# A dilated sliding-window attention and mixer kernel: batch 1 loaded ahead of the second channel weight, the first channel weight in three tiles, scores over 64 rows

## The chip, the cores and the metric

The kernel runs on one core of a Trainium2 chip. The metric is the device time of one execution in microseconds (us). TensorE (PE) multiplies matrices and transposes, VectorE (DVE) and ScalarE (ACT) work on vectors and can read PSUM (the banks that PE writes), GpSimd (POOL) works on vectors in SBUF alone, and SyncE (SP) issues most transfers. POOL issues some transfers too, in the same order as its vector work. PE is fed by weight loads (PEld) that the profile shows as a row of their own.

## The reference

Eight batches, eight heads, 576 positions, 64 channels a head. The first four heads attend to the last 32 positions, the other four to every fourth of the last 128. The result, 576 x 512 for each batch, goes through a mixer over positions (256 hidden) and one over channels (1536 hidden):

```
scores = scale * np.matmul(q, k.transpose(0, 1, 3, 2))
mask_plain = (rel >= 0) & (rel < window)                    # window = 32
mask_dil = (rel >= 0) & (rel < window * dilation) & (rel % dilation == 0)   # dilation = 4
attn = softmax(where(mask, scores, -1e9));  x = attn @ v
h = np.maximum(xt @ w_tok1, 0.0) @ w_tok2                   # over positions
u = x + h.transpose(0, 2, 1)
h2 = np.maximum(u @ w_ch1, 0.0) @ w_ch2                     # over channels
return u + h2
```

## The kernel before, in words

**Attention.** The heads are taken in pairs, hp 0 and 1 plain, hp 2 and 3 dilated. A pair's keys lie transposed on 128 partitions (kt): 64 channels of one head, then 64 of the other. So do its queries, but in two copies (qz): copy h holds head h's rows and zeros in the other 64, so that a matmul over all 128 rows gives the scores of one head. Plain scores are made in blocks of 128 keys by 160 queries, dilated ones by residue modulo 4 in blocks of 128 by 128; the last 64 positions (512 to 575) are blocks of 64 columns of their own (sm). ACT takes exp from the bank to SBUF (attp, attd); the window is set afterwards by a multiplication on POOL with a constant 0/1 band (`mult(nc.gpsimd, ...)`), or, in batches 0 and 1 (`veiled`), ahead of the exp by a matmul that adds a large negative number (veil). The value step of a head multiplies with v and a column of ones, and DVE divides.

**Turning q and k.** In batches 0 to 2 PE transposes them (`transposes`). From batch 3 on (`by_dma`) SP issues transposing transfers to qta, kra and tta (the last 64 positions), and `place_steps` copies from there into qz and kt: POOL the plain pairs and the tails, DVE the dilated queries and a part of the dilated keys.

**Mixer.** `emit_h1` and `emit_u` make the mixer over positions, uT is u turned (by PE up to batch 2, by DMA after). `gen_main` is the channel mixer: 12 row blocks gp (four matmuls of 512 columns each, line 646), each followed by a relu on ACT or DVE to gt, then the second product yp (line 665, 12 matmuls of 256 columns for each half of a block of 128 positions). The last 64 positions of two batches are handled together in the odd batch (gt, line 637, and yp, line 685). The first channel weight is w3, one tile of 128 x 4 x 1536, loaded in three pieces of 512 columns; row block mb uses columns of piece mb // 4 only:

```
return w3[cb][:, 512 * (mb // 4) + mb % 4:512 * (mb // 4) + 512:4]
```

The second channel weight is w4, one tile in three contiguous pieces; yp uses all three in each group of 12 matmuls.

**Order.** The order of all instructions is written out. `interleave` runs the channel mixer of batch b and counts planner time, about a microsecond of PE a unit, on each piece of it and on each step's own cost; a step whose place has been reached is put in next. So a list such as `value_steps(b + 1, 0.4, 0.95)` places the value steps of batch b + 1 at 0.4, 1.35, ... of batch b's channel mixer. Scores are made two batches ahead (`score_steps(b + 2, 15.0 + late, 2.6)`), values, h1, u and uT one batch ahead. Each engine takes its instructions in this order. PSUM has eight banks: main0 to main2 in turn for gp, gt and yp, sc0 and sc1 in turn for scores, three called fl for value steps, h1, u and transposes.

**Start.** POOL loads w3 in three pieces (line 738) among its casts. After the preparation of batch 0, lines 851 to 871: `gate` is a one-element copy on POOL into the target of a load from what has to land first; the load waits for the copy. The first gate lets w4 (line 854) wait for a piece of w3, the second lets batch 1's q and k wait for w4's first piece:

```
gate(w4a[0:1, 0, 0:1], w3[0][0:1, 512:513])
...
gate(l32[(1, "t")][0:1, 0, 0:1], w4[0][0:1, 0:1])
...
```

Between the gates stand w4's three loads; behind the second, batch 1's tails, q and k on SP, its casts on POOL, then its v. Batch 1's transposes begin at planner time 12.6, its value steps at 20.3, its uT at 34.8; the first product of batch 0 ends at 10.3.

Of the kernel before, what the change touches and what calls it, by code (L numbers as in the profile page):

```python
# [16 lines left out]
S = 576  # L17
# [14 lines left out]
BLK = 160  # L32
PST = 256
PTL = 4 * PST
PW = PTL + 192
DTL = 512
DW = DTL + 320
# [20 lines left out]
def _np_dtail():  # L58
    p = np.arange(128)[:, None]
    j = np.arange(64)[None, :]  # L60
    reach = WINDOW * DILATION
    out = []
    for k0 in (384, 512):
        rel = (512 + j) - (k0 + p)
        out.append((rel >= 0) & (rel < reach) & (rel % DILATION == 0))
    return np.stack(out, axis=1).astype(np.float16)
# [3 lines left out]
def kernel(  # L70
# [40 lines left out]
    def mult(eng, out, a, b):  # L111
# [4 lines left out]
    CW = 2 * 128 + BLK + 128  # L116
# [4 lines left out]
    dtail = const[:, 256 + BLK:CW].rearrange("p (x y c) -> p x y c", x=1, y=2)  # L121

    veil = fixed("veil", [128, BLK + 128])
# [4 lines left out]
         _np_dtail().reshape(128, 128)], axis=1)  # L128
# [11 lines left out]
    attp = [fixed(f"attp{i}", [128, 2, PW]) for i in range(2)]  # L140
    attd = [fixed(f"attd{i}", [128, 2, DW]) for i in range(2)]
# [7 lines left out]
    w3a = fixed("w3", [128, 4, DCH])  # L149
    w3 = [w3a[:, i] for i in range(4)]  # L150
# [7 lines left out]
    def emit_fixed():  # L158
# [5 lines left out]
        for a in attp:  # L164
            nc.gpsimd.memset(
                a[:, :, 0:PTL].rearrange("p h (b c) -> p h b c", c=PST)[:, :, :, BLK:PST], 0.0)
            nc.gpsimd.memset(a[:, :, PTL:PW], 1.0)
        for a in attd:
            nc.vector.memset(a[:, :, DTL:DW], 1.0)
# [191 lines left out]
    def place_steps(b):  # L361

        halves = [slice(0, 64), slice(64, 128)]

        def tails():
            eng = nc.vector if b == 3 else nc.gpsimd
            for h in range(2):
                eng.tensor_copy(out=qza[halves[h], :, h, 512:S], in_=tta[halves[h], :, 0:64])
            eng.tensor_copy(out=kta[:, :, 512:S], in_=tta[:, :, 64:128])

        def plain(hp):
            nc.gpsimd.tensor_copy(out=natural(kt[hp][:, 0:512]), in_=kra[:, hp].rearrange("p r m -> p m r"))
            for h in range(2):
                nc.gpsimd.tensor_copy(out=natural(qz[hp][halves[h], h, 0:512]),  # L374
                                      in_=qta[halves[h], hp].rearrange("p r m -> p m r"))

        def dil(h):
            nc.vector.tensor_copy(out=qza[halves[h], 2:4, h, 0:512],
                                  in_=qta[halves[h], 2:4].rearrange("p a r m -> p a (r m)"))

        def dil_k():
            for hp in (2, 3):
# [559 lines left out]
```

## Time and profile before

| | |
|---|---|
| median of 3 runs | 297.87 us (297.7 to 298.11) |
| the profiled execution's own time | 297.69 us |
| its span, first to last instruction | 295.8 us |
| granted PE clock | 1.00 |
| PE busy | 280.8 us, 95% |
| POOL busy | 186.2 us, 63% |
| DVE busy | 156.9 us, 53% |
| ACT busy | 136.6 us, 46% |

Times in the views are microseconds from the span's start, those of single instructions in rows of groups are nanoseconds. A row of a group ends with the idle time ahead of it and what ended it. PE's busy time counts each matmul to its modelled end, so matmuls that follow each other overlap in it.

### The profile page before, as it was taken

To read this page: it belongs to the slowest core of one execution; us is meant where nothing else is said; L and a number is where in the kernel's file an instruction comes from. 1 tells how busy PE (TensorE), PEld (TensorE's weight loads), DVE (VectorE), ACT (ScalarE), POOL (GpSimd) and SP (SyncE) were. 2 spreads that over 40 slices of the span, in tenths; PEclk is the share of its full clock that TensorE was granted. 3 is DMA by queue.
4 is the path that set the end of the run, shared out by engine and by line. 5 is a ranking of instruction groups with operands and counts; after the bars stand their busy time and mean duration, and the time that the engine had idled before them with its cause. 6 is when DMAs were issued, how large, how long until landed. Compare 5 with 4: busy or idle time off the path is not lost.

```text
span 295.8 us, 7055 instructions
## 1 busy us (share of the span) xinstructions
PE 280.8 (95%) x2810; PEld 218.7 (74%) x2810; DVE 156.9 (53%) x303; ACT 136.6 (46%) x266; POOL 186.2 (63%) x256
## 2 busy tenths in 40 slices
PE   5698999988999999999999999999999999999994
PEld 2586589976776986698776976797777976896593
DVE  5766347855828637466743555486654364422022
ACT  3763336356663634556346715474355625224500
POOL 6982045538999899959976999679985920000000
PEclk9999999999999999999999999999999999999999
DMA  7999999999958978179987978399965220531032
GB/s 214 264 202 160 207 320 209 289 265 277 242 112 216 289 228 168 31 175 324 229 149 166 323 219 179 59 216 317 196 127 107 73 74 0 82 115 38 0 89 92
DMA packets 103473, 52.09 MB, mean 176 GB/s; under 512 B 71792, under 2 KB 102384, under 8 KB 103440
## 3 DMA queue, kind: packets, MB, share of 16 engines
q1 hardware_dynamic: 99200, 46.55, 63.8%
q0 software_dynamic: 2640, 3.91, 7.5%
q10 hardware_dynamic: 1600, 1.18, 1.3%
q8 instruction: 22, 0.36, 0.5%
q14 instruction: 11, 0.09, 0.1%
HBM read 37.04 MB, written 9.44 MB: 157 GB/s over the span
## 4 chain that ended last, share of the span: by engine, by line
PE 78%; DMA 10%; POOL 6%; issue 3%; ACT 2%; SPq 0%; DVE 0%; POOLq 0%; ACTq 0%
PE gp L646 26%; PE yp L665 25%; PE h1p L513 4%; PE up L525 4%; DMA w<-in_moe_w_ch_dram 4%; PE yp L685 4%; PE sc L407 3%; PE gt L637 3%; DMA l_k<-in_k_dram 2%; DMA l_vn<-in_v_dram 2%; DMA l_q<-in_q_dram 2%; POOL vv L103 1%; PE sm L407 1%; PE h1p L511 1%; PE av L483 1%
## 5 line engine op out<-in xcount | busy, mean ns | idle before, releaser
L665 PE MATMUL yp<-w,gt 128*128 128x256 f16 x756 | 92.2, 273 | 0.0
L107 ACT ACTIVATE gt<-gp 128x512 f16<-128x512 f32 x76 | 45.4, 597 | 78.5 <-PE gp L646 78.2
L665 PEld LDWEIGHTS <-gt 128*128 128x128 f16 x768 | 76.8, 106 | 5.2 <-issue 0.3
L646 PEld LDWEIGHTS <-w 128*128 128x128 f16 x384 | 40.0, 114 | 24.4 <-issue 2.0
L113 POOL TENSOR_TENSOR attp<-attp,const 128x1280 f16<-128x1280 f16 (+1 forms) x24 | 36.9, 1564 | 18.1 <-ACT attp L436 18.0
L646 PE MATMUL gp<-utd,w 128*128 128x512 f16 x120 | 45.6, 380 | 0.0
L646 PE MATMUL gp<-utm,w 128*128 128x512 f16 x120 | 45.5, 379 | 0.0
L675 DVE TENSOR_TENSOR o<-yp,u 128x512 f32<-128x512 f32 x31 | 21.2, 688 | 45.1 <-PE yp L665 42.5
L646 PE MATMUL gp<-uT,w 128*128 128x512 f16 x144 | 36.2, 379 | 1.5 <-DMA w<-in_moe_w_ch_dram 0.8
L113 POOL TENSOR_TENSOR attd<-attd,const 128x1024 f16<-128x1024 f16 (+1 forms) x24 | 32.8, 1398 | 0.0
L113 DVE TENSOR_TENSOR xn<-av,rec 128x320 f16<-128x320 f32 x64 | 31.5, 492 | 2.2
L407 PEld LDWEIGHTS <-kt 128*128 128x128 f16 x272 | 22.2, 101 | 5.1 <-issue 1.5
L427 ACT ACTIVATE attp<-sc 128x480 f16<-128x480 f32 x32 | 17.8, 572 | 9.8 <-PE sc L407 9.2
L531 DVE TENSOR_TENSOR u<-up,xn 128x512 f16<-128x512 f32 x26 | 18.0, 691 | 8.1 <-PE up L525 8.1
L374 POOL COPY qz<-qt 64x512 f16<-64x512 f16 x20 | 21.6, 1081 | 0.6
L103 POOL CAST c_q<-l_q 128x512 f16<-128x512 f32 x31 | 18.9, 615 | 4.4 <-DMA l_q<-in_q_dram 4.4
L109 DVE TENSOR_SCALAR gt<-gp 128x512 f16<-128x512 f32 x20 | 13.8, 688 | 12.4 <-PE gp L646 11.9
L103 POOL CAST c_k<-l_k 128x512 f16<-128x512 f32 x29 | 17.7, 613 | 2.8 <-DMA l_k<-in_k_dram 2.6
L456 ACT ACTIVATE attd<-sc 128x512 f16<-128x512 f32 x32 | 17.9, 600 | 2.7 <-PE sc L407 2.5
L407 PE MATMUL sc<-qz,kt 128*128 128x160 f16 (+1 forms) x144 | 18.1, 228 | 1.0 <-DVE kt L315 1.0
L107 ACT ACTIVATE h<-h1p 128x256 f16<-128x256 f32 x29 | 11.1, 383 | 16.5 <-PE h1p L513 16.4
L502 DVE RECIPROCAL rec<-av 128x5 f32<-128x5 f32 x64 | 12.1, 189 | 11.2 <-PE av L499 5.9
(139 smaller groups left out, 487.8 us busy)
## 6 DMA issues: line engine op xcount, KB each, us to landing
out_dram<-o SPq DMA_DIRECT2D x72, 128.0 KB, 3.0
l_q<-in_q_dram SPq DMA_DIRECT2D x15, 512.0 KB, 6.6
l_k<-in_k_dram SPq DMA_DIRECT2D x14, 512.0 KB, 7.0
l_vn<-in_v_dram SPq DMA_DIRECT2D x32, 128.0 KB, 5.6
l_vd<-in_v_dram SPq DMA_DIRECT2D x16, 256.0 KB, 3.8
w<-in_moe_w_ch_dram POOLq DMA_DIRECT2D x6, 512.0 KB, 8.6
lt<-in_q_dram SPq DMA_DIRECT2D x8, 128.0 KB, 4.0
l_vt<-in_v_dram SPq DMA_DIRECT2D x8, 128.0 KB, 3.7
```

What stands on the lines that cost most here:

```text
L103: eng.tensor_copy(out=out, in_=in_)
L107: nc.scalar.activation(out=out, in_=in_, func=AF.Relu)
L109: eng.tensor_scalar_max(out=out, in0=in_, scalar1=0.0)
L113: eng.tensor_tensor(out=out, in0=x, in1=y, op=ALU.mult)
L374: nc.gpsimd.tensor_copy(out=natural(qz[hp][halves[h], h, 0:512]), in_=qta[halves[h], hp].rearrange("p r m -> p m r"))
L407: nc.tensor.matmul(out=out, lhsT=lhsT, rhs=qz[hp][:, h, queries], start=hide is None, stop=True)
L427: nc.scalar.activation(out=blocks[:, h, 0:3, 0:BLK], in_=p[:, 0:3 * BLK].rearrange("p (b c) -> p b c", c=BLK), func=AF.Exp, scale=0.125)
L456: nc.scalar.activation(out=a[:, h, 0:DTL], in_=p, func=AF.Exp, scale=0.125)
L531: nc.vector.tensor_tensor(out=u16(b, s), in0=blocks4(p), in1=blocks4(xn[b][:, s]), op=ALU.add)
L646: nc.tensor.matmul(out=p, lhsT=w3_block(cb, mb), rhs=uT[(b, cb)][0], start=(i == 0), stop=(i == 3))
L665: nc.tensor.matmul(out=p[:, c], lhsT=gta[:, mb, a0:m0 + 512:4] if half else gta[:, mb, a0:a0 + 128], rhs=w4[mb][:, c], start=(mb == 0), st ...
L675: nc.vector.tensor_tensor(out=blocks4(o32), in0=blocks4(p), in1=u16(b, s), op=ALU.add)
```

## The change

**Batch 1 first.** The gate for batch 1's q and k now hangs on w3's first piece, and its v loads follow its k at once. The third piece of w3 is loaded after a gate on the second. w4's three loads are issued by POOL after 14 of batch 1's 17 casts. In batch 0's channel mixer, batch 1's transposes start at planner time 2.9 instead of 12.6, its value steps at 11.2 instead of 20.3, h1 at 15.0 instead of 24.2, u at 17.6 instead of 29.0, uT at 25.0 instead of 34.8; the loads of batch 2's q and k come at 19.0.

**Three tiles.** w3 is three tiles of 128 x 4 x 512, one for each piece.

**Scores over 64 rows.** From batch 3 on qz is not used. `scores_twin` makes the scores of two pairs in one burst: each matmul reads 64 partitions of kt or kra as weights and the same 64 of qta or tta, and the two heads of a pair follow each other, into different banks. A burst takes six banks (two sc, three fl, one main). Its first step issues all matmuls, its second the exps and the masks. The plain queries stand in qta by residue, so the exps of the plain pairs read the bank in permuted order. `place_steps` keeps only the copies to kt, all on POOL. There are two bursts a batch, 4.5 planner units apart (4.2 for batch 3).

**Tails.** For all batches the last 64 positions' probabilities of all four pairs go to one tile attt, and in the plain pairs too they are two blocks of 64 columns, against keys 384 to 511 and 512 to 575; the fourth plain block is 128 wide instead of 160. attt is set to one by a single memset.

The core of the diff:

```diff
-    w3a = fixed("w3", [128, 4, DCH])
-    w3 = [w3a[:, i] for i in range(4)]
+    w3 = [fixed(f"w3_{i}", [128, 4, 512]) for i in range(3)]
...
-        for a in attd:
-            nc.vector.memset(a[:, :, DTL:DW], 1.0)
+        nc.vector.memset(attt, 1.0)
...
         def tails():
-            eng = nc.vector if b == 3 else nc.gpsimd
-            for h in range(2):
-                eng.tensor_copy(out=qza[halves[h], :, h, 512:S], in_=tta[halves[h], :, 0:64])
-            eng.tensor_copy(out=kta[:, :, 512:S], in_=tta[:, :, 64:128])
+            nc.gpsimd.tensor_copy(out=kta[:, :, 512:S], in_=tta[:, :, 64:128])
...
+    def tail_scores(b, hp, p, c0):
+        for h in range(2):
+            for x in range(2):
+                c = c0 + 128 * h + 64 * x
+                v0 = BLK + 128 * (hp // 2) + 64 * x
+                score(b, hp, h, p[:, c:c + 64], slice(384 + 128 * x, 512 + 128 * x), slice(512, S),
+                      veil[:, v0:v0 + 64] if veiled(b, hp) else None)
...
+    def scores_twin(b, g):
+        tags = (("sc", 2), ("sc", 2), ("fl", 3), ("fl", 3), ("fl", 3), ("main", 3))
+        ps = [bank(*tags[i], f"sc_{b}_{g}_{i}") for i in range(6)]
+        small = ps[4:6]
+        def twin(hp, banks, c, keys, queries):
+            for h in range(2):
+                rows = slice(64 * h, 64 * h + 64)
+                nc.tensor.matmul(out=banks[h][:, c], lhsT=keys(rows), rhs=queries(rows), start=True, stop=True)
+        for j in range(2):
+            hp = 2 * g + j
+            if g == 0:
+                for kb in range(3):
+                    twin(hp, ps[2 * j:2 * j + 2], slice(BLK * kb, BLK * kb + BLK),
+                         lambda rows: kt[hp][rows, 128 * kb:128 * kb + 128],
+                         lambda rows: qta[rows, hp, :, 32 * kb:32 * kb + 40])
+            else:
+                for r in range(4):
+                    twin(hp, ps[2 * j:2 * j + 2], slice(128 * r, 128 * r + 128),
+                         lambda rows: kra[rows, hp, r], lambda rows: qta[rows, hp, r])
...
+                    exp(plain_blocks(hp)[:, h, 0:3, 0:BLK].rearrange("p b (m r) -> p b m r", r=4),
+                        p[:, 0:3 * BLK].rearrange("p (b r m) -> p b m r", r=4, m=40))
...
-    gate(w4a[0:1, 0, 0:1], w3[0][0:1, 512:513])
...
-    gate(l32[(1, "t")][0:1, 0, 0:1], w4[0][0:1, 0:1])
+    gate(l32[(1, "t")][0:1, 0, 0:1], w3[0][0:1, 0, 0:1])
...
+    load_v(1)
+    gate(w3[2][0:1, 0, 0:1], w3[1][0:1, 0, 0:1])
+    load_w3(2)
     casts1 = cast_steps(1)
-    for i in (0, 1, 2, 3, 4, 5, 7, 6, 8):
+    for i in (0, 1, 2, 3, 4, 5, 7, 6, 8, 9, 10, 11, 12, 13):
         casts1[i]()
...
...
-                                 ((12.6, 14.8), (14.0, 16.8), (16.2, 18.6), (17.6, 20.2)))
+                                 ((2.9, 5.0), (4.2, 6.5), (6.6, 8.9), (7.6, 10.2)))
...
-            va = value_steps(1, 20.3, 0.7)
-            steps += mix_steps(1, 24.2, 27.0, 29.0, 34.8, 1.1)
+            va = value_steps(1, 11.2, 0.6)
+            steps += mix_steps(1, 15.0, 16.5, 17.6, 25.0, 1.1)
...
-            steps += score_steps(3, 22.2, 2.8) + at(9.0, 0.6, cast_steps(3))
+            steps += score_steps(3, 25.2, 4.2) + at(9.0, 0.6, cast_steps(3))
...
-                steps += at(2.0, 0.6, cast_steps(b + 2)) + score_steps(b + 2, 15.0 + late, 2.6)
+                steps += at(2.0, 0.6, cast_steps(b + 2)) + score_steps(b + 2, 16.6 + 1.25 * late, 4.5)
```

More of the change, by code (lines that the diff above doesn't have):

```diff
@@ L458, in scores_dil @@
         p = small_bank(b, hp)
[L459 to L466 removed]
+        tail_scores(b, hp, p, 0)
```

207 lines of the change are left out of this document (120 added, 87 removed).

## The prediction

> **What bounds the kernel now.** I read the page's first part, then busy time in stretches, then the chain and the timelines of the stretches that stand out.
>
> ```profile
> span 295.8 us, 7055 instructions
> PE 280.8 (95%) x2810; PEld 218.7 (74%) x2810; DVE 156.9 (53%) x303; ACT 136.6 (46%) x266; POOL 186.2 (63%) x256
> ```
>
> TensorE (PE) is busy 95%, no other engine above 63% (the weight loads, PEld, overlap it). Where is it idle? Busy time in stretches (core's length, then PE, with its instructions):
>
> ```profile
> 48.00:52.00 4.00, 3.58 (x65) 3.40 (x63) 2.58 (x6) 2.59 (x6) 2.03 (x4) 1.00 0.98 201
> ...
> 56.00:58.00 2.00, 1.71 (x28) 1.50 (x25) 1.93 (x7) 0.38 (x1) 1.10 (x2) 1.00 1.04 313
> ...
> 64.00:72.00 8.00, 6.06 (x72) 4.80 (x71) 3.36 (x7) 6.87 (x16) 4.04 (x6) 1.00 0.85 248
> ```
>
> ```profile
> 174.00:204.00 30.00, 29.85 (x295) 23.35 (x292) 18.84 (x32) 15.64 (x30) 25.38 (x33) 1.00 0.77 189
> ...
> 239.00:265.50 26.50, 26.50 (x239) 20.48 (x236) 12.26 (x27) 9.53 (x16) 0.00 (x0) 1.00 0.28 65
> ```
>
> In the steady stages (174 to 204 is batch 4's channel product with the work for batches 5 and 6) PE has no hole and the granted clock is 1.00: only less matmul work shortens them. Batch 6's stage, with no scores to make, is 3.5 us shorter. Between 28 and 70.8, the stage in which batch 1 is prepared, PE is idle 3.41 us:
>
> ```profile
> 28.00:70.80 42.80, 39.39 (x434) 1.00 1.02 249
> ```
>
> **The size of a hole.** A matmul's busy time holds its latency; the next starts much sooner (timeline of PE):
>
> ```profile
> 48.71 0.19 PE L405 MATMUL sm<-veil,const 128*128 128x64 f16 x1
> 48.74 0.19 PE L407 MATMUL sm<-qz,kt 128*128 128x64 f16 x1
> ```
>
> 64 columns take 0.19 us but come 0.03 apart, so each visible hole hides 0.16 us more. The stretch has eight, so it can give at most 3.41 + 8 x 0.16 = 4.7 us.
>
> **Part 1: the first weight in three tiles.** The first product starts like this (timeline, all engines):
>
> ```profile
> 27.99 0.58 ACT L101 COPY uT<-tpu 128x512 f16<-128x512 f16 x1 [0.38 <-PE tpu L559]
> 28.02 0.38 PE L646 MATMUL gp<-uT,w 128*128 128x512 f16 x1
> 28.22 0.69 DVE L103 COPY uT<-tpu 128x512 f16<-128x512 f16 x1 [0.33 <-PE tpu L559]
> ...
> 29.19 2.11 PE L646 MATMUL gp<-uT,w 128*128 128x512 f16 x9 [0.80 <-DMA w<-in_moe_w_ch_dram]
> ```
>
> In the chain the awaited load is the third one, issued at 18.69 and landing 10.37 later, at 29.06:
>
> ```profile
> 18.69 10.37 DMA w<-in_moe_w_ch_dram
> ...
> 39.50 2.62 PE yp L665 x24
> ```
>
> The first four row blocks need columns of the first piece only, so with a tile each this wait goes. What is late next is uT: its last two copies end at 27.99 + 0.58 = 28.57 and 28.22 + 0.69 = 28.91. The fourth matmul (29.19 + 2 x 0.215 = 29.62) comes at about 28.95: 0.67 gained. Against it batch 0's scores get two more 64-column matmuls per plain pair, each with its veil (2 x 2 x 2 x 0.03 = 0.24, less 0.1 for two blocks narrowed from 160 to 128 columns) and a larger constant load, say 0.1. The one memset of attt is longer on DVE:
>
> ```profile
> L169 DVE MEMSET attd<- 128x640 f16 x2 | 1.2, 592 | 0.2
> ...
> L742 DVE TENSOR_SCALAR veil<-const 128x288 f16<-128x288 f16 x1 | 0.2, 236 | 1.3 <-DMA const<-consts 1.3
> ```
>
> By elements it is 2560/640 x 0.592 = 2.4 us in place of 1.2; DVE waits 1.3 us for the constants there, so the 1.2 more is hidden. Without that cover it would cost up to 1.2. Part 1: **+0.4** (-0.8 to +0.7).
>
> **Part 2: batch 1 ahead of the second weight.** The loads now (POOL, then SP's queue):
>
> ```profile
> 26.56 0.18 POOL L734 COPY w<-w 1x1 f16<-1x1 f16 x1 [4.54 <-DMA w<-in_moe_w_ch_dram]
> 27.04 1.64 POOL L854 DMA_DIRECT2D w<-in_moe_w_ch_dram  x3 [0.30 <-POOL w L734]
> 32.05 0.17 POOL L734 CAST lt<-w 1x1 f32<-1x1 f16 x1 [3.37 <-DMA w<-in_moe_w_ch_dram]
> 38.88 0.61 POOL L103 CAST c_t<-lt 128x512 f16<-128x512 f32 x1 [6.65 <-DMA lt<-in_k_dram]
> ...
> 49.94 0.61 POOL L103 CAST vv<-l_vt 64x512 f16<-64x512 f32 x1 [0.52 <-DMA l_vt<-in_v_dram]
> ```
>
> ```profile
> 32.26 0.61 SPq L197 DMA_DIRECT2D lt<-in_q_dram  x1
> ```
>
> Pieces of a weight land 2.5 us apart (26.5, 29.06), so the first piece lands at about 24.0. Batch 1's loads are then issued at 24.2, not 32.26. Today they queue behind the second weight, whose pieces land at 32.0 and about 34.6 and 37.2; from there to batch 1's last needed v cast (49.94) are 12.7 us. After the change they flow from 26.5, with the third piece (2.5) among them: that cast comes at 26.5 + 2.5 + 12.7 = 41.7 and ends at 42.3. Only then does POOL issue the second weight, which is now queued behind 14 casts. As from 27.04, its pieces land 5.0, 7.6 and 10.2 later: 47.3, 49.9, 52.5.
>
> PE reaches the second product when? Of the 42.8 us, 42.8 - 4.7 = 38.1 are work: 10.3 the first product (48 x 0.215), 10.5 the second (eight groups at 1.31; the chain shows 24 in 2.62), 2.2 for batch 2's first two pairs (2 x 0.61, 18 transposes at the 0.0575 of 128 columns, both in part 3), so 15 for batch 1. By the planner's places all of these 15 but the last u blocks and uT (2.3) come before the second product: 28.0 + 10.3 + 12.7 = 51.0. There PE wants the last piece about 0.9 later. So it waits some 0.6 us, or 1.5 with small delays. Batch 1's values, reached at about 41.6, also wait for the cast ending at 42.3; waits for fixed times are not added, the later one covers the earlier. I take 1.3, and 0.7 for tiles evacuated late: 12 relus share ACT and DVE with batch 1's copies, where today yp left these engines free. Of the other holes (4.7 - 0.96 for the first) 3.75 go, 2.0 come: **+1.75** (bounds: +3.5 with all hidden; -2.5 where v or the weight is 4 us later). What is queued behind the new waits: on POOL the gate for the third piece (until 26.5) holds only batch 1's casts, whose first data cannot land before 28; POOL then issues one load, 14 casts, three loads. SP issues batch 1's six q, k and eight v loads in one row, nothing else is due there until the first output. The third piece is wanted at 28 + 6.9 plus the steps ahead of it, past 36; landing at 31 to 36 it is hidden. Batch 2's loads (start_loads) come at about 50, into the second weight's transfer; their first use is some 10 us later by the planner's places, so they cost nothing unless held back by over 2 us.
>
> **Part 3: scores over 64 rows, batches 3 to 7.** Now (PE, batch 4's scores; the start of the next row ends a group):
>
> ```profile
> 126.26 0.37 PE L407 MATMUL sc<-qz,kt 128*128 128x160 f16 x3
> 126.47 0.82 PE L665 MATMUL yp<-w,gt 128*128 128x256 f16 x6
> ...
> 131.22 0.36 PE L407 MATMUL sm<-qz,kt 128*128 128x160 f16 x4
> 131.41 0.39 PE L407 MATMUL sc<-qz,kr 128*128 128x128 f16 x4
> 131.64 0.82 PE L665 MATMUL yp<-w,gt 128*128 128x256 f16 x6
> ...
> 136.70 0.28 PE L407 MATMUL sm<-qz,kt 128*128 128x64 f16 x4
> 136.82 1.48 PE L665 MATMUL yp<-w,gt 128*128 128x256 f16 x12
> ```
>
> ```profile
> L407 PE MATMUL sc<-qz,kr 128*128 128x128 f16 x80 | 7.0, 218 | 0.3 <-ACT attd L456 0.3
> ```
>
> A plain pair costs 2 x 0.21 + 0.19 = 0.61, a dilated one 2 x 0.23 + 0.12 = 0.58, a batch 2.38 (the group above: 16 such matmuls in each of five batches). Every matmul contracts 128 rows of which 64 are zero. The new ones contract 64; the two heads of a pair read different partitions and write different banks. No row shows a 64-row matmul. Bounds: the halves run at once, so 24 pairs cost 6 x 0.07 + 2 x 0.0575 + 4 x 0.03 + 8 x 0.0575 + 4 x 0.03 = 1.23 and a batch gains 1.15; or one after the other, 48 in place of 44, 2.47, and a batch loses 0.09. I take the first, since the two share neither rows nor bank and matmuls 0.03 apart show that issue is no bound. Five batches: 5.7. Nor does a row show a 64-row matmul beside a 128-row one: such a change costs between nothing and the latency above, 0.16, and ten bursts make 20 changes: 0 to 3.2; I take the middle, 1.6.
>
> The Trainium skill, TensorEngine Tiling (Array Packing), says under Key Properties that a change of tiling mode drains the engine, and under Theoretical Speedup that two row tiles bring up to 2x. By the first the whole 3.2 would be paid and the sum be 1.6 us higher; no run here shows it yet.
>
> The two waits of this group for ACT (0.3 visible, 2 x 0.16 behind them) go: I count 0.4. Part 3: **+4.5** (-3.3 to +6.3).
>
> What can take it back are banks: a burst holds six of eight. The exps' prices, and POOL's masks:
>
> ```profile
> L456 ACT ACTIVATE attd<-sc 128x512 f16<-128x512 f32 x32 | 17.9, 600 | 2.7 <-PE sc L407 2.5
> ...
> L583 ACT COPY utd<-utm 128x512 f16<-128x512 f16 x10 | 10.8, 1086 | 4.1 <-DMA utm<-u 4.1
> ...
> L464 ACT ACTIVATE attd<-sm 128x256 f16<-128x256 f32 x16 | 6.1, 384 | 3.2 <-PE sm L407 3.2
> ...
> L101 ACT COPY uT<-tpu 128x512 f16<-128x512 f16 x3 | 1.8, 585 | 2.9 <-PE tpu L559 2.9
> ```
>
> ```profile
> L113 POOL TENSOR_TENSOR attp<-attp,const 128x1280 f16<-128x1280 f16 x12 | 31.9, 2658 | 18.1 <-ACT attp L436 18.0
> L113 POOL TENSOR_TENSOR attd<-attd,const 128x1024 f16<-128x1024 f16 x12 | 25.5, 2126 | 0.0
> ...
> L113 POOL TENSOR_TENSOR attd<-attd,const 128x256 f16<-128x256 f16 x12 | 8.0, 670 | 0.0
> ```
>
> The first burst's four large exps take 0.6 each, the small ones 0.38: the first small bank is free at most 0.45 + 2.4 + 0.77 = 3.6 us after the burst begins. The second burst wants it after its own first 0.46 and five yp groups of 0.65 behind the first burst's 0.65: 4.3. Hidden by 0.7. Masks: 2.66, 1.07 (670 ns scaled to 512 elements), 2.66 for the first burst, 2.13, 2.13, 1.07 for the second, behind the first burst's exps (4.4): they end 16.1 after it starts. The next batch's fifth value step comes 10.9 + 4.6 = 15.5 after it (planner: burst at 17.3, stage end 28.7, bursts 0.3 cheaper than planned; value step at 4.6). The 0.6 between is within the overlap of queued operations; I count nothing, at most 0.6 in each of two batches. POOL loses five copies a batch and takes two small ones from DVE, which loses four. The turned q and k are now read until the second burst; the next turn comes in the next stage, so SP gains no wait. Batches 1 and 2 pay for the narrow blocks like batch 0, 0.14 with veils and 0.07 without: **-0.2**.
>
> **Sum.** 0.4 + 1.75 + 4.5 - 0.2 = 6.45 from the profiled execution's own 297.69 (span 295.8, 1.9 around it; 0.18 under the median 297.87): **291.2**.
>
> **Rivals.**
> A. Switching costs nothing and batch 1 comes with waits of 0.5 instead of 2.0: 291.2 - 1.6 - 1.5 = 288.1. For it: my sum has the second weight only 1.5 us behind PE, less than the error of two estimated landings. Against: 12 relus more on two engines that then hold all of batch 1's copies.
> B. Each change between 64 and 128 rows costs the full latency: 1.6 more, 292.8. For it: nothing in the profile forbids it. Against: score and yp matmuls of different length follow each other without a gap above. (What the Trainium skill, TensorEngine Tiling (Array Packing), Key Properties, states of a mode change is this case.)
> C. The halves do not run at once, so the 64 rows save nothing: part 3 is 0.4 - 0.45 in place of 4.5, 295.7. For it: no row shows such a pair. Against: see part 3.
> D. Slower than before: the plain exps now read their bank in permuted order. If that goes like the permuted copy utd (1086 ns), six exps take 4 x 0.49 + 2 x 0.35 = 2.7 longer; the second burst then waits 2.7 - 0.7 = 2.0 in each of five batches: 301.2. It turns the sum to slower from 2.0 us over six exps, 0.33 each. Against: uT is a permuted copy as well, but reads a bank, and takes 585.
>
> **How the numbers follow.** Forecast 0.48, A 0.25, B 0.11, C 0.10, D 0.06. A measurement of this kernel tells no change from about 0.2% (0.6 us). C lies 2.0 under the time before, so with part 2 low (down to -2.5) half of it stays faster (0.05), 0.03 is within 0.2% and 0.02 slower; of the forecast 0.01 is within. Faster 0.47 + 0.25 + 0.11 + 0.05 = 0.88, same 0.04, slower 0.08. The likeliest case alone spans 289.0 to 293.5. The range 286.6 to 296.2 goes 1.5 beyond A, for part 2 at its upper bound, and 0.5 beyond C; D and the worst of C are left out.
>
> **What would show it.** Right: the first product's second matmul waits for no load; PE's visible idle between 28 and the end of batch 0's stage falls from 3.4 to about 1.5 us; score matmuls in which two heads start within 0.01 us; the stage of batch 4 shorter by about 0.9 us. Wrong: pairs 0.03 to 0.07 apart (C), holes at both ends of every burst (B), plain exps near 1 us and second bursts that wait for ACT (D), more than 2 us of waiting for the second weight at about 51 (part 2).

## The result

The changed kernel takes 294.83 us (median of 4 runs, 294.67 to 295.32); the kernel before, beside it, 297.78 (296.65 to 298.11). The ratio is 0.9908, interval 0.9883 to 0.9933: 2.7 us (2.0 to 3.5) faster by the ratio, 2.95 by the medians, where 6.45 were forecast. The direction and the range hold, the size does not.

The page of the profile after, whose own execution took 295.32, shows the work that went, most of all on DVE (156.9 before) and POOL (186.2):

```profile
span 293.5 us, 7087 instructions
PE 279.5 (95%) x2850; PEld 214.4 (73%) x2850; DVE 132.6 (45%) x279; ACT 134.4 (46%) x266; POOL 165.3 (56%) x227
```

In e11 and e13 of the table below, which are one kernel, seven of twelve executions ran at a mean granted clock of 0.987 to 0.994 and took 294.4 to 298.5 us, the other five 290.2 to 291.9; so the medians of these two cannot be set beside the others, their ratios leave six of the seven out, and why e10 has no such executions no run shows.

Where the time went is seen when the span is cut at the first matmul of each batch's first channel product: stage 0 runs from batch 0's to batch 1's, and so on. Busy time in these stretches (length, then PE, PEld, DVE, ACT, POOL with their instructions; clock, DMA share, GB/s) of the kernel before, batches 0 to 3:

```profile
28.02:69.59 41.57, 38.78 (x431) 31.52 (x429) 23.29 (x48) 19.89 (x41) 16.75 (x30) 1.00 1.02 248
69.59:108.38 38.79, 38.06 (x407) 30.09 (x405) 23.05 (x46) 20.29 (x42) 37.81 (x46) 1.00 0.87 232
108.38:138.13 29.75, 29.60 (x288) 23.18 (x287) 18.58 (x31) 15.64 (x30) 26.42 (x35) 1.00 0.67 165
138.13:173.36 35.23, 34.94 (x349) 27.09 (x347) 17.65 (x33) 16.76 (x32) 30.19 (x36) 1.00 0.95 220
```

and of the changed kernel:

```profile
27.68:71.28 43.60, 39.72 (x444) 31.27 (x442) 23.92 (x49) 20.48 (x42) 17.86 (x31) 1.00 0.92 230
71.28:109.86 38.58, 37.74 (x413) 29.09 (x411) 17.19 (x38) 19.21 (x41) 33.80 (x43) 1.00 0.96 240
109.86:138.56 28.70, 28.70 (x293) 21.98 (x292) 12.74 (x27) 15.11 (x30) 22.14 (x28) 1.00 0.76 175
138.56:172.97 34.41, 34.12 (x352) 25.93 (x351) 14.01 (x29) 16.35 (x32) 25.64 (x30) 1.00 0.92 226
```

Stage 2 is 1.05 shorter, and so is stage 4, which has the same lengths; stage 3 goes from 35.23 to 34.41, and stage 5 likewise. Together these four give 3.72: the 64-row scores of batches 4 to 7. Stage 1, which makes the scores of batch 3, is only 0.21 shorter. Stage 0, which part 2 was to shorten, is 2.03 **longer**; its visible idle time rose from 2.79 (41.57 - 38.78) to 3.88. The 0.34 that are left lie ahead of the first product.

The new score bursts (PE's timeline, changed kernel, batch 6's scores):

```profile
189.54 0.82 PE L735 MATMUL yp<-w,gt 128*128 128x256 f16 x6
190.30 0.64 PE L475 MATMUL sc<-qt,kt 64*128 64x160 f16 x14
...
191.04 3.45 PE L735 MATMUL yp<-w,gt 128*128 128x256 f16 x30
194.43 0.62 PE L475 MATMUL sc<-qt,kr 64*128 64x128 f16 x16
194.88 0.28 PE L475 MATMUL sc<-tt,kt 64*128 64x64 f16 x8
195.10 1.17 PE L735 MATMUL yp<-w,gt 128*128 128x256 f16 x9
```

Eight pairs of 128 columns start within 194.88 - 194.43 = 0.45 us, 0.056 a pair: the time of one such matmul of 128 rows (0.0575 in the prediction). Two heads do run at once. With the prediction's 0.03 for 64 columns the four pairs of the next row are issued in 0.12, by 195.00; yp comes at 195.10, so 0.10 goes to the change back. Six yp in the first row end at 189.54 + 6 x 0.109 = 190.19, the burst begins at 190.30: 0.11 for the change there. The ten bursts are alike in this.

The holes of stage 0 (PE's timeline, changed kernel). The first row is the start of the first product, which waits for no load any more; the others are the nine rows with the longest waits (in brackets the idle time and what ended it):

```profile
27.68 3.48 PE L716 MATMUL gp<-uT,w 128*128 128x512 f16 x14
...
32.96 0.40 PE L309 MATMUL tp_k<-const,c_k 128*128 128x128 f16 x4 [0.62 <-POOL c_k L102]
33.52 0.40 PE L309 MATMUL tp_q<-const,c_q 128*128 128x128 f16 x4 [0.16 <-POOL c_q L102]
38.58 0.40 PE L309 MATMUL tp_k<-const,c_k 128*128 128x128 f16 x4 [0.42 <-POOL c_k L102]
42.89 0.19 PE L390 MATMUL sm<-veil,const 128*128 128x64 f16 x1 [0.32 <-ACT attd L455]
49.05 0.28 PE L559 MATMUL av<-vv,attd 128*128 128x65 f16 x4 [0.29 <-ACT h L106]
50.29 0.28 PE L576 MATMUL h1p<-xn,w1t 128*128 128x256 f16 x1 [0.35 <-DVE xn L112]
52.50 0.38 PE L601 MATMUL up<-h,w 128*128 128x512 f16 x1 [0.30 <-DVE h L108]
...
68.42 0.39 PE L392 MATMUL sm<-qz,kt 128*128 128x128 f16 x6 [0.79 <-ACT attp L428]
71.05 0.39 PE L392 MATMUL sm<-qz,kt 128*128 128x128 f16 x6 [0.51 <-ACT attp L428]
```

With 0.16 of hidden latency each, as in the prediction, that is 1.68 for three waits for batch 1's casts, 1.90 for four waits on the chain of banks and evacuations, and 1.62 for batch 2's small scores. With two short holes that are not shown (0.11 and 0.02) the stage's eleven holes cost 3.88 + 11 x 0.16 = 5.64; its seven in the kernel before cost 2.79 + 7 x 0.16 = 3.91. These 1.73 and the 13 more matmuls (0.2 by the prediction's prices) are nearly all of the 2.03. The last kind was there before, in one hole, and is untouched by the change (kernel before):

```profile
66.64 0.36 PE L407 MATMUL sm<-qz,kt 128*128 128x160 f16 x4 [0.80 <-ACT attp L427]
```

In this execution the second weight was no wait: yp came just late enough. In another of the same kernel (e5 below), whose first product starts 0.6 later, it is the other way round: none of the three waits for casts is there, the weight is waited for, and the stage is as long (43.70):

```profile
56.92 0.60 PE L735 MATMUL yp<-w,gt 128*128 128x256 f16 x4 [1.56 <-DMA w<-in_moe_w_ch_dram]
```

Why it lands so late is seen in SP's own queue and POOL's timeline of the changed kernel. SP issues batch 2's loads (start_loads) from 40.27 on, directly behind the last of batch 1's v loads:

```profile
40.27 0.61 SPq L196 DMA_DIRECT2D lt<-in_q_dram  x1
...
44.17 0.68 SPq L190 DMA_DIRECT2D l_k<-in_k_dram  x1
```

and POOL the second weight only at 42.45, into the middle of them:

```profile
41.89 0.61 POOL L102 CAST vv<-l_vt 64x512 f16<-64x512 f32 x1 [1.08 <-DMA l_vt<-in_v_dram]
42.45 1.62 POOL L934 DMA_DIRECT2D w<-in_moe_w_ch_dram  x3
...
56.57 0.62 POOL L102 CAST c_k<-l_k 128x512 f16<-128x512 f32 x1 [8.24 <-DMA l_k<-in_k_dram]
```

The group of the weight's three loads says how long each took from issue to landing:

```profile
L934 POOL DMA_DIRECT2D w<-in_moe_w_ch_dram x3: 543/551/551, 42.5 to 43.5; - x3
...
DMA to landing us min/median/max: 7.7/10.1/12.5
```

The last piece lands at 43.5 + 12.5 = 56.0. Last, the waits of stage 1 (PE, changed kernel), and the masks on POOL that they are for:

```profile
78.66 0.20 PE L554 MATMUL av<-vv,attp 128*128 128x65 f16 x1 [0.30 <-POOL attp L112]
...
81.99 0.20 PE L562 MATMUL av<-vt,attt 128*128 128x65 f16 x1 [0.23 <-POOL attt L112]
```

```profile
69.38 2.60 POOL L112 TENSOR_TENSOR attp<-attp,const 128x1280 f16<-128x1280 f16 x1 [8.25 <-ACT attp L437]
71.94 0.67 POOL L112 TENSOR_TENSOR attt<-attt,const 128x256 f16<-128x256 f16 x1
72.55 1.44 POOL L102 CAST vv<-l_vn 128x256 f16<-128x256 f32 x4
...
75.62 0.40 POOL L102 CAST vt<-l_vx 128x256 f16<-128x256 f32 x1
75.98 2.62 POOL L112 TENSOR_TENSOR attp<-attp,const 128x1280 f16<-128x1280 f16 x1
```

POOL idles 8.25 us, and then does eight casts of batch 2's v (72.55 to 75.98, 3.4 us) between the first mask and the next.

### The profile page after: what moved, and what is told of

Its sections match the earlier page's. It is cut to its first block, busy times and chain, and to the rows that moved or that the text cites. A ratio compares the mean times of both kernels' runs of the same rounds, so it can differ in the third digit from the quotient of the medians.

```text
span 293.5 us, 7087 instructions
## 1 busy us (share of the span) xinstructions
PE 279.5 (95%) x2850; PEld 214.4 (73%) x2850; DVE 132.6 (45%) x279; ACT 134.4 (46%) x266; POOL 165.3 (56%) x227
## 4 chain that ended last, share of the span: by engine, by line
PE 84%; DMA 5%; POOL 3%; DVE 3%; ACT 2%; issue 1%; POOLq 0%; ACTq 0%
PE yp L735 28%; PE gp L716 24%; PE h1p L578 4%; PE up L590 4%; PE yp L755 4%; DMA l_k<-in_k_dram 4%; PE gt L707 3%; PE sc L475 2%; DMA const<-consts 2%; DVE xn L112 1%; PE h1p L576 1%; PE sc L392 1%; POOL vv L102 1%; PE av L559 1%; PE av L554 1%
## 5 line engine op out<-in xcount | busy, mean ns | idle before, releaser
L735 PE MATMUL yp<-w,gt 128*128 128x256 f16 x756 | 86.8, 273 | 0.0
L735 PEld LDWEIGHTS <-gt 128*128 128x128 f16 x768 | 78.5, 106 | 5.9
L112 POOL TENSOR_TENSOR attp<-attp,const 128x1280 f16<-128x1280 f16 x12 | 31.4, 2613 | 38.8 <-ACT attp L499 30.5
L716 PE MATMUL gp<-uT,w 128*128 128x512 f16 x144 | 38.4, 379 | 0.0
L112 POOL TENSOR_TENSOR attd<-attd,const 128x1024 f16<-128x1024 f16 x12 | 25.3, 2123 | 0.0
L108 DVE TENSOR_SCALAR gt<-gp 128x512 f16<-128x512 f32 x20 | 13.7, 687 | 11.2 <-PE gp L716 10.8
L392 PEld LDWEIGHTS <-kt 128*128 128x128 f16 x144 | 12.1, 105 | 4.8 <-issue 2.2
L499 ACT ACTIVATE attp<-sc 128x480 f16<-128x480 f32 (+1 forms) x30 | 13.4, 526 | 2.1 <-PE sc L475 2.1
L112 POOL TENSOR_TENSOR attt<-attt,const 128x512 f16<-128x512 f16 (+1 forms) x14 | 14.2, 1016 | 0.0
L605 DVE TENSOR_TENSOR u16t<-up,xn 64x512 f16<-64x512 f32 x7 | 4.8, 690 | 19.8 <-PE up L601 19.8
L499 ACT ACTIVATE attd<-sc 128x512 f16<-128x512 f32 x20 | 10.3, 602 | 6.6 <-PE sc L475 6.6
```

The costliest lines, as they stand in the source:

```text
L108: eng.tensor_scalar_max(out=out, in0=in_, scalar1=0.0)
L112: eng.tensor_tensor(out=out, in0=x, in1=y, op=ALU.mult)
L392: nc.tensor.matmul(out=out, lhsT=lhsT, rhs=qz[hp][:, h, queries], start=hide is None, stop=True)
L499: nc.scalar.activation(out=out, in_=in_, func=AF.Exp, scale=0.125)
L716: nc.tensor.matmul(out=p, lhsT=w3_block(cb, mb), rhs=uT[(b, cb)][0], start=(i == 0), stop=(i == 3))
L735: nc.tensor.matmul(out=p[:, c], lhsT=gta[:, mb, a0:m0 + 512:4] if half else gta[:, mb, a0:a0 + 128], rhs=w4[mb][:, c], start=(mb == 0), st ...
```

## The experiments

The theory after the result: part 2 itself brings waits that the sum did not have (H). Two rivals: part 2 gains 1.75 as forecast and the loss lies in the 64-row scores (F, in e1 and e2); a removed wait comes back at the next input that arrives at its own time, so that no single step is to blame (L). From e6 on each expectation says itself what H and L stand for there. What each expects of a run is quoted.

Each run's median, its ratio to the kernel before that ran beside it, and from its profiled execution the lengths of stages 0 and 1 and the sum of stages 2 to 5, cut as above:

| run | median us | ratio (95%) | stage 0 | stage 1 | 2 to 5 |
|---|---|---|---|---|---|
| before | 297.78 | | 41.57 | 38.79 | 129.95 |
| changed | 294.83 | 0.9908 (0.9883-0.9933) | 43.60 | 38.58 | 126.23 |
| e1 old order | 293.81 | 0.9900 (0.9879-0.9921) | 41.15 | 38.75 | 126.22 |
| e2 order alone | 299.19 | 1.0085 (1.0054-1.0117) | 42.43 | 38.63 | 130.24 |
| e3 tiles alone | 296.79 | 1.0003 (0.9985-1.0020) | 41.53 | 38.80 | 129.95 |
| e4 heads apart | 299.64 | 1.0100 (1.0070-1.0130) | 42.02 | 39.33 | 130.13 |
| e5 changed, again | 294.94 | 0.9925 (0.9900-0.9950) | 43.70 | 38.61 | 126.24 |
| e6 small bank | 294.86 | 0.9927 (0.9903-0.9951) | 41.98 | 39.73 | 126.23 |
| e7 old order, small bank | 292.85 | 0.9861 (0.9836-0.9886) | 41.15 | 38.94 | 126.23 |
| e8 v ahead | 293.56 | 0.9885 (0.9861-0.9909) | 44.05 | 37.29 | 126.22 |
| e9 gate batch 2 | 293.58 | 0.9878 (0.9849-0.9907) | 42.28 | 38.59 | 126.24 |
| e10 all three | 290.94 | 0.9787 (0.9760-0.9813) | 41.66 | 37.29 | 126.24 |
| e11 weight sooner | 293.58 | 0.9779 (0.9745-0.9814) | 40.71 | 37.30 | 126.23 |
| e12 old order repaired | 292.36 | 0.9850 (0.9824-0.9876) | 41.46 | 38.19 | 126.21 |
| e13 as e11, again | 295.65 | 0.9836 (0.9786-0.9885) | 42.23 | 37.30 | 126.22 |

e1 to e4 ran side by side, so did e5 to e8, e9 to e11, and e12 with e13; between these groups ratios are compared. The time ahead of stage 0 is in no column: the first product starts between 26.65 and 28.63, and 0.6 apart in two executions of the changed kernel.

**e1, e2, e3: the parts taken apart.** e1 is the changed kernel with the old order of loads and steps, so without part 2:

```
+    gate(w4a[0:1, 0, 0:1], w3[1][0:1, 0, 0:1])
+    for i in range(3):
+        nc.gpsimd.dma_start(out=w4a[:, 4 * i:4 * i + 4], ...)
+    gate(l32[(1, "t")][0:1, 0, 0:1], w4[0][0:1, 0:1])
...
-                                 ((2.9, 5.0), (4.2, 6.5), (6.6, 8.9), (7.6, 10.2)))
+                                 ((12.6, 14.8), (14.0, 16.8), (16.2, 18.6), (17.6, 20.2)))
```

> The changed kernel with part 2 undone: gates, load order and batch 0's planner places of the kernel before; three tiles, attt and the 64-row scores stay. Theory H (batch 1's early steps bring more waits into batch 0's stage than they take away; by the stage starts of the two traces part 2 costs some 2 us): about 292.6 us, 2.2 below the changed kernel, and the stage of batch 0 about 2 us shorter. Rival F (part 2 gains 1.75 as forecast, and the missing gain lies in the 64-row scores): about 296.6, slower than the changed kernel.

e2 is the kernel before with the three tiles and part 2, its scores as they were:

```
-    gate(l32[(1, "t")][0:1, 0, 0:1], w4[0][0:1, 0:1])
+    gate(l32[(1, "t")][0:1, 0, 0:1], w3[0][0:1, 0, 0:1])
...
+    load_v(1)
+    gate(w3[2][0:1, 0, 0:1], w3[1][0:1, 0, 0:1])
+    load_w3(2)
```

> The kernel before with the three tiles and part 2's load order and places; its scores and tails stay as before. H: the tiles gain about 1 and the order loses 2 to 2.7, so 298.8 to 299.5, slower than before. F: 297.8 - 0.4 - 1.75 = 295.6.

e3 is the kernel before with the three tiles alone:

```
-    w3a = fixed("w3", [128, 4, DCH])
+    w3 = [fixed(f"w3_{i}", [128, 4, 512]) for i in range(3)]
```

> The kernel before with the first channel weight in three tiles and nothing else (the gate reads the second tile instead of column 512). My forecast for the tiles alone was 0.67, without the costs of the longer tails: 297.1. By the traces, where the third matmul of the first product starts at 28.3 instead of 29.4: 296.7.

Measured: 293.81, 299.19, 296.79. Part 2 alone (e2 against e3, side by side) costs 2.4 us by the medians and 1.9 between the profiled executions, of which 0.9 lies in stage 0 and 0.9 ahead of it. Inside the changed kernel (against e1) the cost is 1.0 to 1.1 by the medians and 0.1% to 0.25% by ratios whose intervals overlap, though stage 0 is 2.45 longer in the profiles. So its size is open; in neither place is it a gain, and F fails. e1 itself came 1.2 above the 292.6 that H expected. The scores with their tails (e1 against e3) give 2.98. In the profiles e1's stages 0 to 5 are 4.16 shorter than e3's, but its first product starts 1.49 later; whether the longer tails have a part in that, no run shows. The three tiles give nothing that can be told from zero (ratio within 0.2%), though the first product starts without a wait. The next fixed time swallows what they gain. In e3's trace (PE) two transposes of batch 1 wait for POOL's casts: tp_k starts 0.3 after the six yp ahead of it are issued (40.20 + 6 x 0.109 = 40.85), and tp_q waits visibly:

```profile
40.20 0.82 PE L664 MATMUL yp<-w,gt 128*128 128x256 f16 x6
41.17 0.40 PE L309 MATMUL tp_k<-const,c_k 128*128 128x128 f16 x4
41.72 0.40 PE L309 MATMUL tp_q<-const,c_q 128*128 128x128 f16 x4 [0.16 <-POOL c_q L103]
```

**e4: do the heads share the array?** The changed kernel, but each burst makes all of head 0's scores and then all of head 1's:

```
-            for h in range(2):
+            for h in (one,):
...
+        for one in range(2):
```

> The changed kernel with each burst's matmuls in another order: all of head 0 of both pairs, then all of head 1, so that no two neighbours read different halves. If the pairs run at once as the trace's equal starts say: 5 x 1.15 more, about 300.5. If their gain came from elsewhere (no zero rows to read, copies gone): unchanged, 294.8.

Measured: 299.64, the whole gain gone and more. A dilated burst now lasts from 131.94 to 133.08, 1.14 in place of 0.67 (PE, e4):

```profile
131.94 0.62 PE L475 MATMUL sc<-qt,kr 64*128 64x128 f16 x8
...
133.08 6.74 PE L736 MATMUL yp<-w,gt 128*128 128x256 f16 x60
```

The 1.14 is about the price before of two dilated pairs, 2 x 0.58. The gain is that of two halves at once, and it hangs on the order, in which matmuls of the two halves alternate. The fewer rows by themselves give nothing.

**e5: the changed kernel again**, to set its weight wait and its spread beside e6 to e8.

> The changed kernel as it is, beside the other three and the kernel before on one chip, to have its ratio under the same conditions: 0.99 of the kernel before.

Measured: 294.94, with 1.56 of visible wait for the weight in its profiled execution and none in the first one, which has the waits for casts instead. Which of the two waits appears hangs on when PE gets there against landings that also move.

**e6, e7: the small scores' bank.** Batch 2's first small blocks go to a bank of another kind, so that they need not wait for the exp that frees one of two; e7 does the same in the old order, for batch 1's small blocks too.

```
-        return bank("main", 3, f"sm_{b}_{hp}") if b == 0 else bank("sc", 2, f"sm_{b}_{hp}")
+        return bank("main", 3, f"sm_{b}_{hp}") if b == 0 or (b == 2 and hp < 2) else bank("sc", 2, f"sm_{b}_{hp}")
```

> The changed kernel, in which the small score blocks of batch 2's plain pairs take a main bank instead of one of the two sc banks. Theory H (the holes at 67 and 70 us, 0.96 + 0.68, come because three score steps in a row share two sc banks, and PE waits for ACT's exp): these two holes go, 1.3 to 1.6 us less than the changed kernel. Rival L (stage 0's end is set by transfers and POOL, so that a hole that goes comes back later): the time stays.

> Part 2 undone (as in the first run: old gates, old places) and the small score blocks of batch 1 and of batch 2's plain pairs in main banks. H: the holes at 49 (0.66) and 65 (0.96) of that order go, 1.2 to 1.6 us less than part 2 undone alone, about 0.985 of the kernel before. L: stays at 0.990.

Measured: e6 294.86, no change. Stage 0 is 1.7 shorter than in e5, stage 1 is 1.1 longer: PE arrives sooner at masks that are no sooner done, and in that execution also waits 1.12 for the weight. e7 measured 292.85, 0.4% below e1's ratio, which looks like the gain that H expected; but its stages 0 and 1 are not shorter than e1's (41.15 and 38.94, against 41.15 and 38.75). The two holes that H named (0.49 at 49.72 and 0.80 at 66.28 in e1) are gone; instead there are two waits for ACT near the end of stage 0 (0.09 visible at 65.16 and 0.27 at 68.18) and two for batch 1's casts, none of which e1 has (the latter: PE, e7):

```profile
42.02 0.40 PE L309 MATMUL tp_k<-const,c_k 128*128 128x128 f16 x4 [0.34 <-POOL c_k L102]
42.58 0.40 PE L309 MATMUL tp_q<-const,c_q 128*128 128x128 f16 x4 [0.16 <-POOL c_q L102]
```

Its first product starts 0.83 sooner than e1's, which is more than the whole difference of the two profiled executions (0.64). So in the old order, too, the removed waits come back (L), and no stage shows a gain of this edit.

**e8: batch 2's v ahead.** Its loads and casts some 5 us sooner, in the 8 us in which POOL idles:

```
-            steps += [(19.0, 0.0, start_loads), (24.0, 0.0, lambda: load_v(2))]
+            steps += [(19.0, 0.0, start_loads), (19.1, 0.0, lambda: load_v(2))]
...
-            steps += at(24.5, 0.5, casts[:9]) + at(34.0, 0.3, casts[9:])
+            steps += at(24.5, 0.5, casts[:9]) + at(29.5, 0.3, casts[9:])
```

> The changed kernel with batch 2's v loads placed right behind its q and k (19.1 instead of 24.0) and its last eight casts at 29.5 instead of 34.0, ahead of the first mask. H: POOL, idle from 61 to 69 us in the changed kernel, then has them behind it when the masks come, and the holes at 78 to 82 us (0.46 + 0.41 + 0.40, value steps waiting for masks) go: 1.0 to 1.3 less. L: unchanged.

Measured: 293.56, 0.4% below e5. Stage 1 falls from 38.61 to 37.29. That is the gain of batch 3's scores, which the masks had hidden; POOL's masks follow each other now (e8):

```profile
69.15 2.61 POOL L112 TENSOR_TENSOR attp<-attp,const 128x1280 f16<-128x1280 f16 x1 [4.17 <-ACT attp L437]
...
72.36 2.61 POOL L112 TENSOR_TENSOR attp<-attp,const 128x1280 f16<-128x1280 f16 x1
```

**e9: batch 2's loads behind the weight.** A small write from the weight's first piece into their target holds them back:

```
+    new_qk(2)
+    gate(l32[(2, "t")][0:1, 0, 0:1], w4[0][0:1, 0:1])
```

> The changed kernel, but batch 2's query and key loads wait, by a small write of the first element of w4's first piece into their target, until that piece has landed; so they no longer come ahead of the second weight in the DMA's order. Theory H (batch 2's loads, which ran ahead of the second weight's, are what delays it): w4's last piece lands at about 52.5 us instead of 56 to 57, the wait of yp for it (0 to 1.7 us, by execution) goes, stage 0 is about 1.2 shorter: about 293.7, ratio about 0.988 to the kernel before. Theory L (it comes back as the wait for batch 2's casts, which then start later): within 0.3% of the changed kernel, 294.5 to 295.

Measured: 293.58, 0.5% below e5 and 0.3% below the first runs of the changed kernel, by ratios of different groups. The weight's loads (e9, the same group as above) now take about as long as the three that the prediction was scaled from (5.0, 7.6 and 10.2):

```profile
L934 POOL DMA_DIRECT2D w<-in_moe_w_ch_dram x3: 541/548/551, 41.2 to 42.3; - x3
...
DMA to landing us min/median/max: 5.2/7.9/10.3
```

The last piece lands at 42.3 + 10.3 = 52.6, and yp does not wait. The Trainium skill, DMA: Bandwidth & Descriptors, says under Queues, rings and completion order that each transfer engine takes turns, packet by packet, between the queues that have work for it. The runs agree in so far as the weight, issued by POOL, is slowed by loads in SP's queue; each piece lands 2.2 to 2.5 us later after its issue in the changed kernel than in e9.

Not all of e9's gain is the weight's. The stretch from the last batch's first product to the end is 29.88 to 29.89 in the profiles of the four kernels with this gate (e9, e10, e11, e13) and 30.36 to 30.40 in the other eleven; the last matmul and the last output landing come at the same place in all. These 0.5 us lie in the program's closing instructions, and why the gate shortens them no run shows. Nor was the wait the same before: against the first profile of the changed kernel, which did not wait for the weight, stage 0 of e9 is shorter because only one short wait for batch 1's casts is left (0.08 visible at 36.56).

**e10: all three repairs at once**, the edits of e6, e8 and e9.

> Three repairs at once on the changed kernel: the small score block of batch 2's first heads in the main bank, batch 2's values loaded ahead with the casts at 29.5, and the gate of the run before on batch 2's loads. H (the holes add: 1.6 at the small scores, 1.2 of masks, 1.2 of the weight, all within the first 82 us, each repaired one no longer swallowed by the next): about 291.0, ratio about 0.979. L (the next fixed time swallows most): 293 to 294, ratio above 0.985.

Measured: 290.94, ratio 0.9787 (six executions from 290.5 to 291.75). That is 1.4% below the changed kernel (e5's ratio). The three alone gave 0, 0.4 and 0.5%. That together they give more than their sum, because no next wait is left to swallow each one, is what L would say; but each of the ratios is known to about 0.25% only, and an excess of 0.5% is within what their errors leave open. Stage 1 has hardly a hole (e10, stages 0 and 1):

```profile
27.19:68.85 41.66, 39.51 (x444) 31.36 (x442) 23.90 (x49) 19.99 (x42) 20.00 (x39) 1.00 0.96 237
68.85:106.14 37.29, 37.22 (x408) 28.94 (x408) 17.01 (x38) 19.32 (x42) 31.65 (x35) 1.00 0.91 231
```

**e11: the weight sooner**, issued after 9 instead of 14 of batch 1's casts, on top of e10. Batch 1's h1, u and uT steps are moved too: not earlier, as the expectation says, but 1.4 to 3.0 planner units later, so the weight is not the only change.

```
-    for i in (0, 1, 2, 3, 4, 5, 7, 6, 8, 9, 10, 11, 12, 13):
+    for i in (0, 1, 2, 3, 4, 5, 7, 6, 8):
...
+    for i in (9, 10, 11, 12, 13):
```

> The three repairs, and the second weight's loads issued after 9 instead of 14 of batch 1's casts, the steps of batch 1 laid some 2 us earlier to match. H (what still bounds the first stage is the landing of the weight and the casts around it): about 1 us below the three repairs, some 290. L (the first 55 us are bound by the DMA's whole traffic, or by the chain of batch 1's steps): no less than the three repairs within 0.3%.

Measured: a ratio of 0.9779, the same as e10 within the intervals, stage 0 shorter by 0.95 in its profile. Not settled as a gain.

**e12, e13: is the order worth anything?** e12 puts the repairs that apply on the old order (on e7, batch 2's v sooner); e13 is e11's kernel again beside it.

```
-            steps += at(24.0, 0.0, [lambda: load_v(2)])
+            steps += at(21.6, 0.0, [lambda: load_v(2)])
...
-            steps += at(24.5, 0.5, casts[:9]) + at(34.5, 0.3, casts[9:])
+            steps += at(24.5, 0.5, casts[:9]) + at(29.5, 0.3, casts[9:])
```

> The changed kernel with the old order of batch 1 and the second weight, with the repairs that apply there: the small score blocks of batch 1 and of batch 2's first heads in the main bank, batch 2's values loaded and cast some 5 us sooner. Theory H (the new order is worth something of its own, as the prediction's part 2 said, some 1 to 2 us, once its waits are repaired): 292 to 292.5, about 0.983 of the kernel before, the masks' waits near 80 us gone and stage 1 some 1 us shorter, but 1 to 1.5 us above the new order repaired. Theory L (the order is worth nothing, only the waits were): within 0.6 us of the new order repaired, some 291.

> The new order with its three repairs and the second weight's loads after 9 casts, run again beside the old order repaired. H: about 290.5, 0.977 to 0.979 of the kernel before, 1 to 1.5 us below the old order repaired. L: within 0.6 us of it.

Measured: e12 292.36 (0.985). Against e10, from another group, the new order repaired is 0.6% better, 1.4 by medians, and the intervals just miss each other (0.9813 and 0.9824). But 0.5 of it are the closing instructions that go with e9's gate. In the profiles e10's stage 0 is 0.20 longer than e12's, and its stage 1 is 0.90 shorter, since e12 still waits there for batch 1's uT (0.74 visible at 70.92): 0.70 for the order. e13 beside e12 does not settle it: 0.9836 with a wide interval. Its profiled execution lost 1.5 in stage 0 against e11's, most of it in one row (PE, e13):

```profile
47.54 0.19 PE L562 MATMUL av<-vt,attt 128*128 128x65 f16 x1 [0.99 <-POOL vt L102]
```

The last of batch 1's v loads, issued by SP at 37.54 beside the weight's three (37.78 to 38.85), is what POOL's cast waits for until 47.09; in e11, the same kernel, that cast is done at 43.6. So this wait comes and goes by execution.

## Why the prediction was right or wrong

| part | forecast us | measured us |
|---|---|---|
| 1, three tiles | +0.4 (0.67 without the tails' costs) | -0.1 +- 0.5 (e3, which has no such costs) |
| 2, order | +1.75 | -2.4 (e2 to e3); -1.0 to -1.1 by medians, -0.2 to -0.7 by ratios (changed to e1) |
| 3 and the tails | +4.5 - 0.2 | +2.98 (e1 to e3); stages 2 to 5 alone 3.72 |

**Part 1** was right in what it removes (the second matmul follows at once) and wrong in what is late next. I named uT's last copies; the casts of batch 1 come after them. e3's stage 0 shows it: the wait of 0.96 goes, and 0.30 for uT and 0.63 for two casts come. End to end no gain is shown; up to 0.4 is not excluded.

**Part 3** was right in its mechanism and nearly in its price. "The halves run at once" is shown by the starts and by e4. A change between 64 and 128 rows was put at 0.08, the middle of two bounds for want of a row, and measured 0.10 each way; that it came so near is luck. The rest of the sum holds: the bursts last 0.74 and 0.67 with the change back, and 0.1 each goes to the change in: 1.61 in place of 2.38, a gain of 0.77. In stages 2 and 4 a wait for ACT goes too (29.75 - 29.60 = 0.15 visible, 0.31 with its latency): 1.08 by this, 1.05 measured. In stages 3 and 5 the visible idle time of 0.29 stays, and 0.8 is measured. The mean is 0.93 a batch, where the sum had 4.5 / 5 = 0.9. What failed is "five batches": batch 3's share lies in stage 1, and there POOL's masks for batch 2 were a bound that I had reckoned only for the steady stages. e8 gives it back.

**Part 2** is the step that failed, as "of the other holes 3.75 go, 2.0 come": a gain of 1.75 was forecast, and the runs show none, and a loss of 2.4 where the order stands without the 64-row scores (e2). In the first profile 2.8 went (3.75 less 0.96 for a hole at batch 2's small scores that stayed) and 4.5 came: 1.68, 1.90, 0.67 for a second hole at those scores, and 0.27 for the short one of 0.11. Four things in it:
- *3.75 go.* Batch 2's small scores were among them, though no edit touches their steps or their bank. They stayed, and with the new one they are 1.62 in two holes. e6 takes them away.
- *2.0 come, casts.* I had checked that batch 1's last v cast came in time (41.7 forecast, 41.89 measured) and not its first ones. PE reaches the transposes of q and k early, and three waits for them cost 1.68 in the first profile and nothing in e5. No term of the sum held that.
- *0.7 for tiles evacuated late* measured 1.90, four holes on DVE and ACT.
- *1.3 for the second weight.* The landing was put at 10.2 after the issue. "Batch 2's loads come at about 50" is the error. It dates SP's issues by PE's place in the plan. But SP went on without a wait from batch 1's v loads and issued them from 40.27 on, the first three ahead of the weight and the rest beside it; the last piece took 12.5 and landed at 56.0 instead of 52.5. With these loads held back (e9) it is 10.3 and 52.6. The wait itself was 0 or 1.7 by execution (1.56 visible in e5 and 0.16 behind it), so the 1.3 was a fair size by luck.

The bound of -2.5 for part 2 covered what e2 shows.

**What would show it.** The first product without a load wait, starts within 0.01 and a stage of batch 4 shorter by about 0.9 (1.05) came as named. The visible idle time between 28 and 70.8 was to fall from 3.4 to about 1.5. It did not (changed kernel):

```profile
28.00:70.80 42.80, 39.17 (x434) 30.82 (x433) 23.75 (x49) 19.68 (x41) 17.14 (x30) 1.00 0.93 233
```

42.80 - 39.17 = 3.63. Of the signs of being wrong none came as named; the second weight was waited for 0 to 1.7, not over 2.

**The rivals.** A fails on both its conditions. B's price, 0.16 a change, is above the 0.10 measured. The Trainium skill, TensorEngine Tiling (Array Packing), says under Key Properties that a change of mode drains the array; the trace agrees that there is a price, and shows that it is 0.10, less than the 0.16 of a matmul's latency that is otherwise hidden. C is refuted by the starts, and e4 is what it looks like. D fails: the exps that read their bank in permuted order (attp, 480 elements) cost no more for an element than the others (attd, 512; changed kernel, all forms of line 499: minimum, median and maximum in ns):

```profile
L499 ACT ACTIVATE attp<-sc x30: 415/568/589, 98.0 to 225.2; 128x480 f16<-128x480 f32 x20, 128x256 f16<-128x256 f32 x10
...
L499 ACT ACTIVATE attd<-sc x20: 591/600/616, 102.5 to 228.8; 128x512 f16<-128x512 f32 x20
```

Why the gain of one part appears and that of another does not is shown by e3, e6, e7 and e8. In the first 82 us PE meets three things that come at their own times: batch 1's casts, the second weight, batch 2's masks. What is gained ahead of one was lost at the next in e3 and e6, and e8, which moves the last, kept its gain. After 110 us there is none, and there the sum held to 0.03 a batch in the mean.

Whether the order, once its waits are repaired, has a worth of its own stays open. By stages 0 and 1 of the profiles the new order is ahead of e12 by 0.70 (e10), 1.64 (e11) and 0.13 (e13, the same kernel as e11), and e12 has been tuned less. The 1.75 of the forecast is not shown.

## What to carry to other kernels

Date a transfer by the queue that issues it: a queue with no wait of its own runs far ahead of the engine whose plan holds the call, and can put its loads ahead of an urgent one. Where several inputs come at times of their own, price a removed wait together with the next one, and repair the last first. A change in a stage without such inputs can be summed from instruction starts: here the sum had 0.9 a batch, and 0.8 and 1.05 were measured. And compare stages, not only medians: a median that falls can hide a stage that did not change (e7).

## What was not expected of the hardware

A matmul over 64 rows beside one over the other 64 cost nothing when they alternated (0.056 us for a pair of 128 columns), and a change between 64 and 128 rows 0.10 us each way, alike in all ten bursts. ACT's permuted reading of a bank cost nothing (568 ns for 480 elements, 600 for 512 in the other exps), where the permuted copy from SBUF took 1086 for 512. The time until batch 0 is prepared differs by execution of the same code: the first product starts at 27.68 in one profile of the changed kernel and at 28.29 in the other, and over all the kernels here between 26.65 and 28.63, which hides effects of half a microsecond in single runs. The gate of e9 shortens the closing instructions by 0.5 us, and no run shows why.
